# Retention and a SwiGLU block in float32 on one core: ring tiles named once and kept, in place of a new tile at every turn

## The chip, the core and the metric

The kernel runs on one core of a Trainium2 chip. A core has five engines with instruction streams of their own: TensorE (PE; its weight loads are listed as PEld), VectorE (DVE), ScalarE (ACT), GpSimd (POOL) and SyncE (SP), which here issues nearly all DMA transfers. [...] The metric is the device time of one execution in microseconds; smaller is better. The kernel before takes 652.57 us, the median of 3 runs (651.63 to 652.96).

## The reference

Two computations follow each other. The first is a retention recurrence over 4 batches, 8 heads, 768 positions and 64 columns per head; its output is turned into 3072 rows of 512 columns, which the second, a SwiGLU block with 1536 inner columns, takes as x.

```python
def _attn_ref(q, k, v):                      # q, k, v: (4, 8, 768, 64)
    gamma = 1.0 - 2.0 ** (-5.0 - np.arange(H, dtype=np.float32))
    scale = 1.0 / np.sqrt(D)
    for t in range(S):
        state = gamma[None, :, None, None] * state + np.einsum('bhd,bhe->bhde', k[:, :, t], v[:, :, t])
        y[:, :, t] = scale * np.einsum('bhd,bhde->bhe', q[:, :, t], state)

def _moe_ref(x, w_gate, w_val, w_out):       # x: (3072, 512)
    g = x @ w_gate                           # (512, 1536)
    silu = g * (1.0 / (1.0 + np.exp(-g)))
    val = x @ w_val
    return (silu * val @ w_out).astype(np.float32)   # w_out: (1536, 512)
```

Everything is float32.

## The kernel before

**Segments.** The 3072 rows are worked in four segments of 768 rows: three chunks of 128 rows for each of two batches. A segment has an up stage (x times the gate and value weights, 12 steps f of 128 inner columns, whose results go to `hT`) and a down stage (hT times `w_out`, 12 steps f of six matmul groups, one per chunk, accumulated in six PSUM banks). In the down stage of a segment the retention of the next one is computed as well: its matmuls stand between the groups of the down projection (L766), and its results are written into the next segment's x. Segment 0 is different: its retention runs first (to about 31 us), its up stage multiplies plainly (`plain`, L891 to L898, and `plain_part` for the first two steps), and beside it the weights are brought in, changed and stored in device memory in the form in which segments 1 to 3 load them (L490, L567, L1120).

**Splits.** TensorE multiplies in the type float32r. So that little is lost, every operand is split into three parts that are added again by three times as many matmuls. One split is three instructions on three engines. For weights and hT they are `near_a` (ScalarE, L967: part 0 from x), `near_b` (VectorE, L970: part 1 from part 0 and x) and `near_c` (part 2 from parts 0 and 1; GpSimd, L973; for hT VectorE, L407, by the function `both`). For x and the weights `w_out` in segment 0 they are `far_a` (L976), `far_b` (L979 on GpSimd, or L407) and `far_c` (L983). The matmuls run over the parts in the order 0, 1, 2.

**The products of the later segments.** In segments 1 to 3 the up stage of one f is seven products (`up3`, L1066): one product is part 0, 1, 2 with two matmuls each (L1060 to L1064), and the seven use seven sums of weights, in three groups of three, three and one (`GROUPS`). A group is one split: two of 768 columns in a tile of the ring "g" and one of 256 columns in a tile of the ring "o". Between the products ScalarE copies banks (L1077 to L1079) before the next product writes to them, and computes the silu (L1078, L1081).

**The rings.** `item` (L955) gives the tile into which a split goes:

```python
    k = turns[kind]
    turns[kind] += 1
    slots = {"g": 4, "o": 3}[kind]
    t = place(f"{kind}item{k}", {"g": 3 * 2 * TH, "o": 3 * DM}[kind], R12,
              tag=f"{kind}{k % slots}")
```

`place` (L409) makes a tile. A tile with the tag of an earlier one gets the same bytes, and what first writes to the new tile waits for all accesses to the old one, of whatever part. Ring "g" has four buffers of 3 x 768 columns, ring "o" three of 3 x 512. In the trace all tiles of a ring are called `gitem` or `oitem`. Users are `near_0` (L877, segment 0's up stage, 512 columns per part), `group` (L1036), `h_split` (L1089, hT, 768 columns per part) and `w_load` (L1102, the weights `w_out`: a DMA of part 2 in segment 0, L1107, followed by far_a to far_c, and of all three parts later, L1109). One call with `other` puts a tile of 3 x 512 over buffer g2. The buffers g0 to g3 hold raw weights (`rawp`) earlier in segment 0.

**x.** The split x of a segment lies in two tiles with the tags "xa" (four sums) and "xb" (three). Segment 0's x is the tile x0 over "xa"; `first`, over "xb", holds changed weights. `begin_x` (L990) makes two new tiles for each later segment:

```python
    xs_of[s] = [place(f"{n}{s}", 3 * o * KH * TH, R12, tag=n).rearrange(
        "p (a o k t) -> p a o k t", a=3, o=o, k=KH) for n, o in (("xa", 4), ("xb", 3))]
```

**Order.** Each piece of work is registered with a key and a due time (`at`, L448), but the order in which the instructions are issued is a list written out by hand, `PLAN` (L50 to L236), which `run` (L452) follows key by key. So each engine's instruction order is fixed; an engine runs its own in this order, and one that waits holds back what stands behind it on that engine.

Of the kernel before, what the change touches and what calls it, by code (L numbers as in the profile page):

```python
# [11 lines left out]
R12 = mybir.dt.float32r  # L12
# [9 lines left out]
DM = H * D  # L22
DFF = 1536
NC = DM // P
NF = DFF // P
L = 3
TH = L * P
NSEG = B * NCK // (2 * L)
KH = NC // 2
# [347 lines left out]
def tile_retnet_swiglu(  # L377
# [31 lines left out]
    def place(name, n, dtype=F32, **kw):  # L409
        return consts.tile([P, n], dtype, name=name, **kw)  # L410

    def f32(t):
        return t.bitcast(F32)

    XA, XB = 3 * 4 * KH * TH, 3 * 3 * KH * TH
    UNIT = 7 * KH * P
    hT = consts.tile([P, NF, 2, TH], F32, name="hT")
    X0 = place("x0", XA, R12, tag="xa").rearrange(
        "p (a i c t) -> p a i c t", a=3, i=2, c=NC)
    first = place("first", XB, tag="xb")  # L420
    rawp = {i: place(f"rawp{i}", 3 * 2 * TH, tag=f"g{i}") for i in (0, 1, 3)}
    loads = place("loads", 3 * UNIT + 256)
# [287 lines left out]
    def x_of(c):  # L710
        i, j = c // NCK % 2, c % L
        return [X0[:, a, i, :, ts(j, P)] for a in range(3)]

# [163 lines left out]
    def near_0(f, n):  # L877
        kind, part = divmod(n, 3)
        if part == 0:
            near_w[f, kind] = item("o", DM, (f, kind) == (1, 1))  # L880
        o = near_w[f, kind]
        o = [o[:, i] for i in range(3)]
        x = wt[f][:, ds(B22 if kind else B21, 2)].rearrange("p a b -> p (a b)")
        if part == 0:
            near_a(o, x)
        elif part == 1:
            near_b(o, x)
        else:
            near_c(o)

    def plain(f, kind, i):  # L891
        o = banks[2 * kind + i][:, :TH]
        w = near_w[f, kind]
        for a in range(3):
            for b in range(NC):
                nc.tensor.matmul(o, w[:, a, ts(b, P)], X0[:, a, i, NC - 1 - b],  # L896
                                 start=a == b == 0, stop=a == 2 and b == NC - 1,
# [11 lines left out]
    def plain_part(f, j, kind):  # L909
        o = part_of(f, j)[0][kind]  # L910
        w = near_w[f, kind]
        for a in range(3):
            for b in range(NC):
                nc.tensor.matmul(o, w[:, a, ts(b, P)], X0[:, a, :, NC - 1 - b, ts(j, P)],  # L914
                                 start=a == b == 0, stop=a == 2 and b == NC - 1,
# [35 lines left out]


    turns = {"g": 0, "o": 0}

    def item(kind, n, other=False):  # L955
        if other:
            t = place("oitem", 3 * DM, R12, tag="g2")
            return t.rearrange("p (a b) -> p a b", a=3)
        k = turns[kind]
        turns[kind] += 1  # L960
        slots = {"g": 4, "o": 3}[kind]
        t = place(f"{kind}item{k}", {"g": 3 * 2 * TH, "o": 3 * DM}[kind], R12,
                  tag=f"{kind}{k % slots}")
        return t[:, : 3 * n].rearrange("p (a b) -> p a b", a=3)

    def near_a(o, x):
        act(o[0], x, AF.Copy, scale=CUT / FAR)  # L967
# [17 lines left out]
    xs_of = {}  # L985
# [2 lines left out]
    st_x = tmp[:, ds(4 * TA, 4 * KH * P)].rearrange("p (m k t) -> p m k t", m=4, k=KH)  # L988

    def begin_x(s):  # L990
        xs_of[s] = [place(f"{n}{s}", 3 * o * KH * TH, R12, tag=n).rearrange(
            "p (a o k t) -> p a o k t", a=3, o=o, k=KH) for n, o in (("xa", 4), ("xb", 3))]

    def bring_y(z, h, i, c):
        y = banks[R0 + c][half[h], ds((2 * z + i) * 2 * HC, 2 * HC)]
# [40 lines left out]
    def group(f, g):  # L1036
        a, n = GROUPS[g]
        n *= KH * P
        src = blocks[f % 3][:, ds(a * KH * P, n)]
        o = ups[f, g] = item("o" if g == 2 else "g", n)  # L1040
        return [o[:, i] for i in range(3)], src
# [47 lines left out]
    def h_split(s, t, f, when):  # L1089
        it = {}  # L1090

        def begin():
            hs[f] = item("g", 2 * TH)
            it["o"] = [hs[f][:, i] for i in range(3)]
            near_a(it["o"], hT[:, f].rearrange("p i t -> p (i t)"))

        a, b, c = when
        at(t + a, f"{s}/h{f}.0", begin)
        at(t + b, f"{s}/h{f}.1", lambda: near_b(it["o"], hT[:, f].rearrange("p i t -> p (i t)")))
        at(t + c, f"{s}/h{f}.2", lambda: near_c(it["o"], pool if s == 0 and f in BY_POOL else both))  # L1100
# [59 lines left out]
    def down_stage(s, t):  # L1160
# [3 lines left out]
        for n in range(6 * NF):  # L1164
# [4 lines left out]
            if nxt and n in PARTS:  # L1169
                what, p = PARTS[n]  # L1170
                d = t + COST[what] + 0.1
                if what == "s":
                    at(t, f"{nxt}/sc{p}", scores_of, p, (R0, R0 + 1) if p else (4, 5))
                    for i in range(2):
                        at(d + 0.1 * i, f"{nxt}/dec{p}.{i}", decayed, p, i)
                        at(d + 0.2 + 0.1 * i, f"{nxt}/q{p}.{i}", scale_q2, p, i)
                    if has_old(nxt, p, 0):
                        at(d + 0.6, f"{nxt}/was{p}.0", decay2, nxt, p, 0)
                    if p == 0:
                        at(d + 0.7, f"{nxt}/begin", begin_x, nxt)  # L1180
                else:
                    k = "ABC".index(what)
                    z = k // 2
                    for i in range(0 if k else 2):
                        at(t - 0.02 + 0.01 * i, f"{nxt}/k{p}.{i}", scale_k2, p, i)
                    at(t, f"{nxt}/{what}{p}", (mix_a, mix_b, mix_c)[k], nxt, p)
                    if k != 1 and has_new(nxt, p, z):
                        at(d, f"{nxt}/new{p}.{z}", keep_state, nxt, p, z)
                    if k == 1 and has_new(nxt, p, 1):
                        at(d + 0.9, f"{nxt}/was{p}.1", decay2, nxt, p, 1)  # L1190
                    for j in range(8 if k else 0):
                        at(d + 0.1 * j, f"{nxt}/y{p}.{z}{j}", bring_y, z, j % 2, j // 2 % 2, j // 4)
                    if k == 2:
                        make_x(d + 1.0, nxt, p, table)
                t += COST[what]
# [44 lines left out]
    t = down_stage(0, end)  # L1240
    for s in range(1, NSEG):
# [8 lines left out]
        t = down_stage(s, t)  # L1250
# [50 lines left out]
```

## Time and profile before

| what | value |
|---|---|
| median of 3 runs | 652.57 us (651.63 to 652.96) |
| the profiled execution, its own time | 652.16 us |
| its span, first to last instruction | 650.4 us |
| mean granted TensorE clock | 0.997 |
| L1062, products of segments 1 to 3 | 1512 matmuls |
| L1125, down projection | 864 matmuls, 208.7 us |
| L896, plain up stage of segment 0 | 480 matmuls, 84.6 us |
| L967 ScalarE near_a | 847 ns (768 columns), 420 (256), 632 (512) |
| DMA read / written | 109.32 / 29.88 MB |

By stretches of the span, in us (busy time of the engines, share of the DMA engines):

| stretch | PE | DVE | ACT | POOL | DMA |
|---|---|---|---|---|---|
| 0 to 31 (segment 0's retention) | 25.93 | 20.29 | 16.30 | 9.57 | 1.00 |
| 31 to 118 (its up stage) | 87.00 | 71.49 | 70.49 | 42.74 | 0.90 |
| 118 to 165 (down stage begins) | 44.53 | 41.08 | 32.32 | 19.06 | 0.82 |
| 165 to 254 (rest of it, then segment 1 up) | 87.16 | 78.63 | 54.22 | 53.32 | 0.60 |
| 254 to 305 (segment 1 up) | 51.00 | 34.19 | 29.10 | 23.52 | 0.56 |
| 535 to 650 (segment 3, up and down) | 111.29 | 67.77 | 44.16 | 35.85 | 0.40 |

A row of the page's list of groups reads: line, engine, operation, output<-inputs by the names of the tiles, shape, count; busy time in us and the mean of one in ns; the engine's idle time just before these instructions and what ended most of it. A row of the timeline reads: start, duration, engine, line, operation, and in brackets the idle time before it and its releaser. Matmuls are pipelined: their starts are measured, their ends are modelled, so that in a steady stream each starts before the one ahead has ended.

### The profile page before, as it was taken

What the parts mean: (1) busy time and instruction counts of PE and PEld (TensorE: products, weight loads), DVE (VectorE), ACT (ScalarE), POOL (GpSimd) and SP (SyncE); (2) the same over time, 40 slices, a digit from 0 to 9 for tenths busy, and PEclk for the clock granted to TensorE, in tenths of its full rate; (3) what the DMA queues carried; (4) which work ended last, traced back from release to release, by engine and by line L of the source; (5) the groups of instructions that cost most, each with busy time, mean ns of one, the idle gap of its engine ahead of it and who ended that gap; (6) DMA issues with size and microseconds to landing.
All of it is one profiled execution on the core that took longest, in us unless ns stands there. A gap on an engine that the chain in (4) does not pass through costs nothing.

```text
span 650.4 us, 14042 instructions
## 1 busy us (share of the span) xinstructions
PE 636.1 (98%) x5576; PEld 579.8 (89%) x5576; DVE 490.3 (75%) x712; ACT 389.5 (60%) x860; POOL 270.9 (42%) x174
## 2 busy tenths in 40 slices
PE   7999999998989999999999999999999999999997
PEld 6899999987769999997878999998777999999886
DVE  4888688798898887675787959767598776778361
ACT  4688788577845555565766555656686554654221
POOL 0544347534445676730102666550003766562000
PEclk8999999999999999999999999999999999999999
DMA  9999898498757544157865540548677444304564
GB/s 325 374 350 336 323 348 283 165 360 283 276 183 302 201 146 166 38 195 261 260 237 205 191 152 20 187 132 294 203 270 264 150 158 163 117 4 157 177 216 147
DMA packets 50050, 140.13 MB, mean 215 GB/s; under 512 B 4928, under 2 KB 17472, under 8 KB 49984
## 3 DMA queue, kind: packets, MB, share of 16 engines
q1 hardware_dynamic: 49552, 138.57, 61.9%
q8 instruction: 44, 0.72, 0.4%
q10 hardware_dynamic: 432, 0.66, 0.3%
q14 instruction: 22, 0.18, 0.1%
HBM read 109.32 MB, written 29.88 MB: 214 GB/s over the span
## 4 chain that ended last, share of the span: by engine, by line
PE 91%; DVE 3%; DMA 2%; ACT 2%; POOL 1%; issue 1%; SPq 0%; ACTq 0%; DVEq 0%; POOLq 0%
PE bank L1062 40%; PE bank L1125 29%; PE bank L896 12%; PE bank L766 5%; PE bank L914 3%; DMA rawp<-in_w_gate_dram 1%; PE bank L636 1%; PE bank L707 1%; ACT chunk_x L996 1%; PE bank L721 1%; POOL oitem L973 1%; PE bank L692 1%; DMA loads<-in_k_n_dram 0%; POOL gitem L973 0%; DMA oitem<-wdn 0%
## 5 line engine op out<-in xcount | busy, mean ns | idle before, releaser
L1125 PE MATMUL bank<-oitem,gitem 128*128 128x512 f32 x864 | 208.7, 395 | 3.2 <-DVE oitem L983 2.9
L1125 PEld LDWEIGHTS bank<-oitem,gitem 128*128 128x128 f32 x864 | 159.3, 188 | 38.6 <-DVE oitem L983 4.4
L973 POOL TENSOR_TENSOR gitem<-gitem 128x768 fp32r<-128x768 f32 x72 | 143.4, 2001 | 105.2 <-DVE gitem L970 102.5
L1062 PE MATMUL bank<-xa,gitem 128*128 128x384 f32 x864 | 162.1, 336 | 0.6 <-ACT tmp L1078 0.3
L1062 PEld LDWEIGHTS bank<-xa,gitem 128*128 128x128 f32 x864 | 150.4, 188 | 3.0 <-ACT tmp L1077 2.2
L973 POOL TENSOR_TENSOR oitem<-oitem 128x256 fp32r<-128x256 f32 (+1 forms) x60 | 66.6, 1114 | 72.3 <-DVE oitem L970 63.7
L970 DVE SCALAR_TENSOR_TENSOR gitem<-gitem,loads 128x768 fp32r<-128x768 f32 x72 | 80.8, 1138 | 13.9 <-ACT gitem L967 10.0
L967 ACT ACTIVATE gitem<-loads 128x768 fp32r<-128x768 f32 x72 | 59.3, 843 | 50.8 <-PE bank L1062 39.3
L1062 PE MATMUL bank<-xb,gitem 128*128 128x384 f32 x432 | 85.4, 335 | 0.1
L896 PE MATMUL bank<-x,oitem 128*128 128x384 f32 x480 | 84.6, 336 | 0.8 <-POOL oitem L973 0.8
L896 PEld LDWEIGHTS bank<-x,oitem 128*128 128x128 f32 x480 | 83.0, 188 | 1.5 <-POOL oitem L973 1.1
L1062 PEld LDWEIGHTS bank<-xb,gitem 128*128 128x128 f32 x432 | 75.9, 188 | 1.0 <-POOL gitem L973 0.6
L970 DVE SCALAR_TENSOR_TENSOR gitem<-gitem,hT 128x768 fp32r<-128x768 f32 x48 | 48.3, 1012 | 26.7 <-ACT gitem L967 26.6
L967 ACT ACTIVATE gitem<-hT 128x768 fp32r<-128x768 f32 x48 | 39.9, 839 | 41.0 <-PE bank L1125 33.4
L996 ACT COPY chunk_x<-bank 64x128 f32<-64x128 f32 x144 | 35.4, 260 | 31.3 <-PE bank L766 17.9
L793 POOL TENSOR_TENSOR loads<-loads,tab 128x512 f32<-128x512 f32 x9 | 13.7, 1522 | 90.9 <-PE bank L766 90.9
L407 DVE SCALAR_TENSOR_TENSOR gitem<-gitem 128x768 fp32r<-128x768 f32 x48 | 46.8, 982 | 0.6
L1062 PE MATMUL bank<-xb,oitem 128*128 128x384 f32 x216 | 43.7, 337 | 0.0
L1062 PEld LDWEIGHTS bank<-xb,oitem 128*128 128x128 f32 x216 | 37.9, 188 | 0.4 <-POOL oitem L973 0.2
L970 DVE SCALAR_TENSOR_TENSOR oitem<-oitem,loads 128x256 fp32r<-128x256 f32 (+1 forms) x42 | 32.8, 786 | 3.7 <-ACT oitem L967 3.6
L979 POOL TENSOR_TENSOR oitem<-oitem 128x512 fp32r<-128x512 f32 x12 | 20.7, 1730 | 28.6 <-ACT oitem L976 28.6
L1079 DVE TENSOR_TENSOR hT<-bank,tmp 128x384 f32<-128x384 f32 x36 | 19.9, 553 | 14.6 <-PE bank L1062 14.6
(112 smaller groups left out, 788.3 us busy)
## 6 DMA issues: line engine op xcount, KB each, us to landing
loads<-wup SPq DMA_DIRECT2D x36, 896.0 KB, 4.7
oitem<-wdnt SPq DMA_DIRECT2D x36, 768.0 KB, 4.4
wdnt<-oitem SPq DMA_DIRECT2D x12, 768.0 KB, 4.6
wup<-first SPq DMA_DIRECT2D x9, 896.0 KB, 5.8
rawp<-in_w_gate_dram SPq DMA_DIRECT2D x12, 512.0 KB, 6.5
rawp<-in_w_val_dram SPq DMA_DIRECT2D x12, 512.0 KB, 5.6
rawp<-in_w_out_dram SPq DMA_DIRECT2D x12, 512.0 KB, 5.7
out_dram<-chunk_x SPq DMA_DIRECT2D x22, 256.0 KB, 2.3
```

Of the source, the lines that this page charges most:

```text
L407: stt(o, x, 1.0, y, op0=mul, op1=op)
L766: nc.tensor.matmul(o, a, b, start=start, stop=True, skip_group_check=True)
L896: nc.tensor.matmul(o, w[:, a, ts(b, P)], X0[:, a, i, NC - 1 - b], start=a == b == 0, stop=a == 2 and b == NC - 1, skip_group_check=True)
L914: nc.tensor.matmul(o, w[:, a, ts(b, P)], X0[:, a, :, NC - 1 - b, ts(j, P)], start=a == b == 0, stop=a == 2 and b == NC - 1, skip_group_che ...
L967: act(o[0], x, AF.Copy, scale=CUT / FAR)
L970: stt(o[1], f32(o[0]), -FAR, x, op0=mul, op1=add)
L973: op(o[2], f32(o[0]), f32(o[1]), op=add)
L979: op(o[1], f32(o[0]), x, op=sub)
L996: copy(cx[half[i], ds(2 * h, 2), c, half[z]], y.rearrange("p (b t) -> p b t", b=2))
L1062: nc.tensor.matmul(o, w[:, a, k], x[:, a, KH - 1 - k], start=start and a == k == 0, stop=a == 2 and k == KH - 1, skip_group_check=True)
L1079: lambda: copy(p5, wb), lambda: tt(h1, x, p5, op=add),
L1125: nc.tensor.matmul(banks[tok], hs[f][:, a, ds(i * TH + u * P, P)], wo[f][:, a], start=f == a == 0, stop=f == NF - 1 and a == 2, skip_group ...
```

## The change

`item` keeps a dictionary `slots` of the tiles it has made, by tag and size. The first turn of each buffer makes a tile; every later turn returns the same tile, cut to the columns asked for. The ring order (four and three buffers, and g2 for `other`) and the bytes are as before. The tile of the tag "xa" is made once, before segment 0, and kept in the list `xab`; the tile "xb" is made at the first `begin_x`, over `first`, and kept as well; `begin_x` then only cuts the two into the views of the segment. No arithmetic, no transfer and no entry of `PLAN` changes. What changes with it is what a first writer's waits go by: accesses to the same bytes of a tile that lives on, in place of the end of all use of the tile that was there before.

```diff
@@ -415,8 +415,8 @@
     hT = consts.tile([P, NF, 2, TH], F32, name="hT")
-    X0 = place("x0", XA, R12, tag="xa").rearrange(
-        "p (a i c t) -> p a i c t", a=3, i=2, c=NC)
+    xab = [place("xa", XA, R12)]
+    X0 = xab[0].rearrange("p (a i c t) -> p a i c t", a=3, i=2, c=NC)
     first = place("first", XB, tag="xb")
@@ -951,17 +951,18 @@
     turns = {"g": 0, "o": 0}
+    slots = {}
 
     def item(kind, n, other=False):
-        if other:
-            t = place("oitem", 3 * DM, R12, tag="g2")
-            return t.rearrange("p (a b) -> p a b", a=3)
-        k = turns[kind]
-        turns[kind] += 1
-        slots = {"g": 4, "o": 3}[kind]
-        t = place(f"{kind}item{k}", {"g": 3 * 2 * TH, "o": 3 * DM}[kind], R12,
-                  tag=f"{kind}{k % slots}")
-        return t[:, : 3 * n].rearrange("p (a b) -> p a b", a=3)
+        k = 2
+        if not other:
+            k = turns[kind] % {"g": 4, "o": 3}[kind]
+            turns[kind] += 1
+        size = {"g": 3 * 2 * TH, "o": 3 * (n if other else DM)}[kind]
+        tag = f"g{k}" if other else f"{kind}{k}"
+        if (tag, size) not in slots:
+            slots[tag, size] = place(f"{kind}item{k}", size, R12, tag=tag)
+        return slots[tag, size][:, : 3 * n].rearrange("p (a b) -> p a b", a=3)
@@ -988,8 +989,10 @@
     def begin_x(s):
-        xs_of[s] = [place(f"{n}{s}", 3 * o * KH * TH, R12, tag=n).rearrange(
-            "p (a o k t) -> p a o k t", a=3, o=o, k=KH) for n, o in (("xa", 4), ("xb", 3))]
+        if len(xab) == 1:
+            xab.append(place("xb", XB, R12, tag="xb"))
+        xs_of[s] = [t.rearrange("p (a o k t) -> p a o k t", a=3, o=o, k=KH)
+                    for t, o in zip(xab, (4, 3))]
```

## The prediction

> **What bounds the kernel now.** I read the page first, then who waited for whom, then the timeline around each place where TensorE steps late. The page:
>
> ```profile
> PE 636.1 (98%) x5576; PEld 579.8 (89%) x5576; DVE 490.3 (75%) x712; ACT 389.5 (60%) x860; POOL 270.9 (42%) x174
> ...
> L973 POOL TENSOR_TENSOR oitem<-oitem 128x256 fp32r<-128x256 f32 (+1 forms) x60 | 66.6, 1114 | 72.3 <-DVE oitem L970 63.7
> L970 DVE SCALAR_TENSOR_TENSOR gitem<-gitem,loads 128x768 fp32r<-128x768 f32 x72 | 80.8, 1138 | 13.9 <-ACT gitem L967 10.0
> L967 ACT ACTIVATE gitem<-loads 128x768 fp32r<-128x768 f32 x72 | 59.3, 843 | 50.8 <-PE bank L1062 39.3
> ```
>
> TensorE is busy for 636.1 of 650.4 us, so all that any change of waits can win is in the other 14.3 us and in matmuls that run late inside "busy" (their ends are modelled). ScalarE, VectorE and GpSimd have room. The last row shows what the change touches: ScalarE's first step of a split (near_a, L967) is idle for 50.8 us before its 72 instructions, mostly for TensorE. The waits, as engine and line, what was waited for, us in total, times, longest:
>
> ```profile
> ACT gitem L967 <- PE bank L1062: 41.6, 27, 3.7
> ACT gitem L967 <- PE bank L1125: 37.0, 17, 4.6
> ...
> ACT oitem L967 <- PE bank L896: 6.9, 6, 1.8
> ```
>
> In 50 cases near_a stands until a matmul has ended. It reads hT, `loads` or `first`, none of them written by TensorE, so what it waits for is room: the tile that had its buffer before must have been read for the last time. Whether that matters is decided by what is queued behind near_a on ScalarE. One place, in order of time:
>
> ```profile
> 510.10 2.07 PE L1062 MATMUL bank<-xa,gitem 128*128 128x384 f32 x11
> ...
> 511.21 0.85 ACT L967 ACTIVATE gitem<-loads 128x768 fp32r<-128x768 f32 x1 [1.31 <-PE bank L1062]
> ...
> 511.97 0.46 ACT L1078 COPY tmp<-bank 128x384 f32<-128x384 f32 x1
> 512.32 0.48 ACT L1079 COPY tmp<-bank 128x384 f32<-128x384 f32 x1
> 512.48 0.47 PEld L1062 LDWEIGHTS bank<-xa,gitem 128*128 128x128 f32 x3 [0.63 <-ACT tmp L1078]
> 512.48 0.62 PE L1062 MATMUL bank<-xa,gitem 128*128 128x384 f32 x2 [0.31 <-ACT tmp L1078]
> ```
>
> near_a starts at 511.21, 0.09 us after the last matmul on the old tile ended (511.13), and the copy that empties the bank (L1078) stands behind it until 511.97. TensorE needs that bank and starts at 512.48 in place of about 512.01. Consecutive matmuls of this line start 0.173 us apart (median); this one came 0.64 us after the one before, and the next 0.28. So the place costs 0.47 + 0.11 = 0.58 us, the 0.11 being a restart that follows every such wait.
>
> **The change part by part.** *Weights and hT (gitem, oitem).* Before, each turn is a new tile over the old one, and its first writer waits for the last access of the old tile whatever part it touched. Kept tiles have their history by the bytes: near_a writes part 0 and needs only the readers of part 0. A product runs part 0, 1, 2 with two matmuls each (L1060 to L1064), so the last reader of part 0 is four matmuls earlier: 4 x 0.173 = 0.69 us. In the down projection (L1125) it is two, 2 x 0.227 = 0.45 us, and in segment 0 (L896, four per part) eight, 8 x 0.173 = 1.39 us. For each near_a that the records show waiting for such a matmul, I took the latest of the earlier reader's end, ScalarE's instruction before and its other waits: some 60 of them could start earlier, by 36 us in total, 0.6 us at the mean. None of this is yet time. It becomes time only where TensorE stalls behind it.
>
> I followed every step of TensorE in these lines that is over 60 ns late back along its releases. Nine have a waiting near_a in the chain (time of the start; stall + restart, us): 125.64: 0.93 + 0.10; 216.47: 0.24 + 0.11; 232.71: 0.17 + 0.10; 248.60: 0.15 + 0.11; 392.91: 0.17 + 0.10; 512.48: 0.47 + 0.11; 538.83: 0.18 + 0.10; 546.66: 0.42 + 0.11; 590.99: 0.18 + 0.11. For the eight after 200 us the head start of 0.3 to 0.7 us is more than the stall, and what is next in the way is the end of the product that the copy reads: at 232.71 near_a moves from 230.71 to 230.02, a second near_a follows it, and the copy L1077, at 232.19 now, could start at 231.75, 0.09 after its product, which ends at 231.66. That is 0.44 earlier for a stall of 0.17. Sum of the eight: 2.83 us.
>
> The first is a longer chain:
>
> ```profile
> 118.67 6.21 PE L896 MATMUL bank<-x,oitem 128*128 128x384 f32 x34
> ...
> 119.27 0.63 ACT L967 ACTIVATE oitem<-loads 128x512 fp32r<-128x512 f32 x1 [1.78 <-PE bank L896]
> ...
> 119.94 0.69 DVE L970 SCALAR_TENSOR_TENSOR oitem<-oitem,loads 128x512 fp32r<-128x512 f32 x1 [2.40 <-ACT oitem L967]
> ...
> 120.66 2.59 DVE L407 SCALAR_TENSOR_TENSOR loads<-loads 128x512 f32<-128x512 f32 x3
> 120.71 1.80 POOL L973 TENSOR_TENSOR oitem<-oitem 128x512 fp32r<-128x512 f32 x1 [3.99 <-DVE oitem L970]
> ...
> 123.17 0.68 DVE L970 SCALAR_TENSOR_TENSOR oitem<-oitem,loads 128x512 fp32r<-128x512 f32 x1
> ...
> 123.94 1.66 POOL L973 TENSOR_TENSOR oitem<-oitem 128x512 fp32r<-128x512 f32 x1 [1.43 <-DVE oitem L970]
> 125.64 0.64 PEld L896 LDWEIGHTS bank<-x,oitem 128*128 128x128 f32 x4 [1.08 <-POOL oitem L973]
> 125.64 0.79 PE L896 MATMUL bank<-x,oitem 128*128 128x384 f32 x3 [0.77 <-POOL oitem L973]
> ```
>
> VectorE is idle for 2.40 us until near_a has run, then works without a gap to 123.86, and GpSimd's part 2 of the last weight ends at 125.59. near_a could start at 117.88, 1.39 earlier, and the chain with it, so the 1.03 us could go. But the down projection of segment 0 follows, at 0.82 DMA share between 118 and 165 us, and its first weight load (L1107, issued at 123.73 behind a reader that does not move) feeds ScalarE at 128.26 and GpSimd until 131.47; VectorE takes that result at 132.81, so 1.34 us are spare there, yet later loads may give some back. Between 0 and 1.03 I take 0.6.
>
> *The waits that are added.* near_b (VectorE, part 1) and near_c (part 2; GpSimd, for hT VectorE) now have readers of their own to wait for, due later than near_a's by a third and two thirds of a product's remainder. For 768 columns: 0.35 and 0.69 us, while near_a itself takes 0.843, so it hides both. For 256 columns: near_a 0.42 and near_b 0.41 against 0.35 and 0.69, hidden. For 512 in segment 0: 0.69 and 1.39 against 0.63 + 0.09 and 0.69 more, just hidden; without that cover VectorE would stand up to 0.35 us, and the hT additions (L1079 to L1081) behind it. As instructions: a wait beyond the first stands in a semaphore instruction of its own. Where such a wait had long been met, the start after the instruction before (which overlaps by the modelled pipeline) came at -79 ns against -82 without it on VectorE, -94 and -94 on ScalarE, -39 and -39 on GpSimd: 0 to 3 ns, and 200 of them cost at most 0.6 us of engines that are idle a quarter of the time. On TensorE more matmuls must report their end; after those that report now the next starts 173 ns later at the median, after the others 174. Cost 0, bounds 0 to 0.1 us.
>
> *x (xa, xb).* The earlier segment's last matmul on xb ends at 291.8, the first write for the next is at 308.9 (445.1 and 467.3 for the one after; x0 134.2, first write to xa1 159.0): at least 17 us apart, so nothing waits and nothing is won. *W loads* write part 2 or all parts; their last reader is the old one: nothing. *The tile over g2* is used once.
>
> Sum: 2.83 + 0.6 = 3.4 us. The profiled execution took 652.16 (650.4 span, 1.8 around it), 0.41 under the median of the runs: **648.8 us**.
>
> **The rivals.** *More.* Segment 0's down projection also stalls at 157.80 (1.85 us), 180.76 and 187.46 (1.36) behind VectorE. If earlier splits loosen these, another 1 to 3 us go: about 646. Against it: VectorE works without a gap from 148.79 to 160.7, started by copies that follow TensorE, and no near_a waits there. *Nothing.* If the dependencies of a kept tile are still taken whole, or near_a's wait goes to the next matmul that reports, all stays: 652.2. For it: nothing in the trace of before shows a kept tile with three parts being rewritten while read; `tmp` and `loads` are rewritten in pieces, and there L1077 starts without regard to the pieces beside it. *Slower: VectorE and GpSimd collide.* L970 on 768 columns takes 0.945 us at the least and 1.890 at the most in segment 1's up stage; the slow ones run beside GpSimd's L973 (1.87). An earlier near_b can move from a free stretch into one of these, 0.945 us late, then near_c and TensorE behind it. Slack on VectorE between 254 and 305 us is 51.0 - 34.2 = 16.8, 2.4 us for each of its seven steps of 7.3, so most are absorbed; if one in six of the 36 steps of the later segments paid 0.945 on TensorE's path, 5.7 us would be lost: 652.2 - 3.4 + 5.7 = 654.5. Four such eat the gain, five or six make it slower by a measurable amount. Against it: in the whole up stages only one stall, at 216.47, ends on GpSimd, and none on VectorE's L970. [...]
>
> **How the numbers follow.** A measurement tells 0.2% (1.3 us) from no change. Chances: forecast (2 to 5 us won) 0.62, more 0.06, nothing or less than 1.3 either way 0.21, slower 0.11 (collisions 0.08, the rest unknown). Faster by over 0.2% is then 0.68. The range goes down to 646.8 (3.86 whole, half a microsecond of five lone restarts of 0.11, 1 us of the first rival) and up to 652.4, into the case of nothing; below and above are left some 0.05 and 0.13.
>
> **What would show it.** Right: near_a's idle before its release by L1062 falls by about 0.6 us each, from 41.6 us; the starts at 512.48 and 546.66 lose their waits for ScalarE; VectorE's near_b at 119.94 comes over a microsecond earlier and 125.64 follows the matmul before it. Wrong: L967 still starts 0.09 us behind the product's last matmul (nothing), or L970's mean rises well over 1138 ns while PEld waits for VectorE or GpSimd (slower). What would upset the sum itself is a stall that moves to a place that near_a never reached.

## The result and the profile after

| | before | after |
|---|---|---|
| median, executions in turn on one chip | 653.36 us (651.63 to 655.14, 12) | 649.13 us (648.11 to 652.34, 12) |
| ratio of after to before | | 0.9941, 95% interval 0.9926 to 0.9955 |
| the profiled execution, its span | 652.16, 650.4 us | 652.34, 650.5 us |
| L1062, now L1065, near_a idle for it | 41.6 us in 27 waits | 24.8 us in 21 waits |

The change takes 0.6% off, some 4 us. Ratios are of fast executions alone; one execution of experiment 9, at 2193.21 us, is left out of its ratio. The profiled execution of the changed kernel is its slowest of the twelve: before 458.31 us TensorE stands for 2.70 us, in a place that has nothing to do with the rings, and its granted clock is one half for 6.83 us around that place (the last section). Times of stages are therefore read from a second profile of the same, unaltered kernel (experiment 10, 648.84 us); the idle times of near_a (31.8 us) and near_b (7.5) below are the same in both.

The line numbers move by one to three: near_a is L968, near_b L971, near_c L974, the products L1065, the copies L1080 to L1082. The rows of the page that answer to those shown of before, from the list of groups of the kernel after (idle time and its releaser at the end):

```profile
L974 POOL TENSOR_TENSOR oitem<-oitem 128x256 fp32r<-128x256 f32 (+1 forms) x60 | 67.7, 1132 | 70.1 <-DVE oitem L971 56.1
L971 DVE SCALAR_TENSOR_TENSOR gitem<-gitem,loads 128x768 fp32r<-128x768 f32 x72 | 81.1, 1143 | 7.5 <-ACT gitem L968 5.8
L968 ACT ACTIVATE gitem<-loads 128x768 fp32r<-128x768 f32 x72 | 59.2, 842 | 31.8 <-PE bank L1065 24.4
```

near_a's idle time went from 50.8 to 31.8 us and near_b's from 13.9 to 7.5, while near_b's mean, 1143 ns against 1138, did not rise. Who waited for whom, in the kernel after (total us, times, longest):

```profile
ACT gitem L968 <- PE bank L1128: 39.7, 15, 7.1
...
ACT gitem L968 <- PE bank L1065: 24.8, 21, 3.0
...
POOL gitem L974 <- PE bank L1065: 15.1, 9, 4.5
...
ACT oitem L968 <- PE bank L896: 2.1, 3, 1.5
```

The waits for the products fell by 16.8 us, 0.62 for each of the 27, and those for segment 0's up stage from 6.9 to 2.1. Counted in matmuls, 20 of the 24 splits of weights from `loads` that waited for a product start exactly four matmuls earlier than before. The waits for the down projection hardly moved: the first row holds the long stall at 458, and in the second profile it is 35.9 us, against 37.0 before, although 11 of 14 splits of hT start two matmuls earlier there; the work ahead of each wait comes earlier too. The third row had been this in the list before:

```profile
POOL gitem L973 <- PE bank L1062: 2.8, 1, 2.8
```

near_c now waits nine times and not once, since it has readers of its own part to wait for. The place that the prediction took as its example, in order of time, in the kernel after:

```profile
511.97 4.34 PE L1065 MATMUL bank<-xa,gitem 128*128 128x384 f32 x23
...
512.84 0.85 ACT L968 ACTIVATE gitem<-loads 128x768 fp32r<-128x768 f32 x1 [1.34 <-POOL gitem L974]
513.59 0.46 ACT L1081 COPY tmp<-bank 128x384 f32<-128x384 f32 x1
...
514.10 2.06 PEld L1065 LDWEIGHTS bank<-xa,gitem 128*128 128x128 f32 x12 [0.21 <-ACT tmp L1081]
514.25 0.48 ACT L1082 COPY tmp<-bank 128x384 f32<-128x384 f32 x1 [0.20 <-PE bank L1065]
```

The pair of products on xa starts at 511.97 here, and in the profile of before at 509.93:

```profile
509.93 2.24 PE L1062 MATMUL bank<-xa,gitem 128*128 128x384 f32 x12
```

From there the two can be laid side by side. near_a came 1.28 us behind that start (511.21 - 509.93) and comes 0.87 behind it now (512.84 - 511.97); the copy behind it came at 2.04 and comes at 1.62, and the 23 matmuls run on as one row where TensorE stood until 2.55 before. The head start is 0.41 us and not the 0.69 of four matmuls: the wait that ends last now is, by the profile, for GpSimd's near_c. That is nearly all of the 0.47 that was lost there: TensorE comes 0.06 us late at 514.11, and a restart of 0.11 is left at 514.39.

The other chain, at the end of segment 0's up stage, in the kernel after:

```profile
117.62 0.63 ACT L968 ACTIVATE oitem<-loads 128x512 fp32r<-128x512 f32 x1 [0.39 <-PE bank L896]
...
118.31 0.69 DVE L971 SCALAR_TENSOR_TENSOR oitem<-oitem,loads 128x512 fp32r<-128x512 f32 x1 [1.04 <-ACT oitem L968]
...
119.03 2.60 DVE L407 SCALAR_TENSOR_TENSOR loads<-loads 128x512 f32<-128x512 f32 x3
...
121.55 0.68 DVE L971 SCALAR_TENSOR_TENSOR oitem<-oitem,loads 128x512 fp32r<-128x512 f32 x1
...
122.31 1.68 POOL L974 TENSOR_TENSOR oitem<-oitem 128x512 fp32r<-128x512 f32 x1 [1.43 <-DVE oitem L971]
```

near_b's idle time there is 1.04 us in place of 2.40, and all that follows on VectorE without a gap comes with it: GpSimd's last part ends at 123.99, or 77.61 us after the first matmul of L896 (at 46.38), against 125.60 - 46.65 = 78.95 before. TensorE no longer stands in front of it.

From the start of every TensorE matmul come the lengths of the stages, from the first matmul of one to the first of the next (us; segment 0's up stage from the first matmul of L896, the last stage to the start of its last matmul):

| stage | before | after (second profile) | difference | the prediction's terms |
|---|---|---|---|---|
| segment 0 up | 87.36 | 86.15 | -1.21 | -1.03 |
| segment 0 down | 67.98 | 67.14 | -0.83 | +0.43 |
| segment 1 up | 89.66 | 88.99 | -0.67 | -0.88 |
| segment 1 down | 60.81 | 61.02 | +0.21 | 0 |
| segment 2 up | 89.47 | 89.15 | -0.32 | -0.27 |
| segment 2 down, without the stall at 458 | 62.70 | 62.72 | +0.02 | 0 |
| segment 3 up | 91.29 | 89.37 | -1.92 | -1.68 |
| segment 3 down | 49.85 | 49.85 | 0.00 | 0 |
| sum | | | -4.72 | -3.43 |

The stall at 458 was 0.42 us in the profile before and 1.87 in the second profile after. It varies from execution to execution and is left out of the row; that the medians differ by 4.2 and the stages by 4.7 is within it. Of the 0.21 of segment 1's down stage, 0.18 are a stall of 0.07 and its restart of 0.11 at 314.

### The profile page after: what moved, and what is told of

Read it like the earlier page. It is cut to its first block, busy times and chain, and to the rows that moved or that the text cites. A ratio compares the mean times of both kernels' runs of the same rounds, so it can differ in the third digit from the quotient of the medians.

```text
span 650.5 us, 14090 instructions
## 1 busy us (share of the span) xinstructions
PE 635.7 (98%) x5576; PEld 581.5 (89%) x5576; DVE 489.6 (75%) x712; ACT 392.4 (60%) x860; POOL 272.3 (42%) x174
## 4 chain that ended last, share of the span: by engine, by line
PE 89%; DMA 4%; DVE 3%; ACT 2%; issue 1%; SPq 0%; ACTq 0%; DVEq 0%
PE bank L1065 40%; PE bank L1128 27%; PE bank L896 13%; PE bank L766 5%; PE bank L914 2%; DMA rawp<-in_w_gate_dram 1%; ACT chunk_x L999 1%; DMA hT<-in_k_n_dram 1%; DMA hT<-in_q_t_dram 1%; DVE oitem L984 0%; DMA loads<-in_v_n_dram 0%; DVE xb L407 0%; PE bank L721 0%; ACT states L865 0%; DVE tmp L407 0%
## 5 line engine op out<-in xcount | busy, mean ns | idle before, releaser
L1128 PE MATMUL bank<-oitem,gitem 128*128 128x512 f32 x864 | 210.9, 398 | 5.6 <-DVE oitem L984 2.9
L1128 PEld LDWEIGHTS bank<-oitem,gitem 128*128 128x128 f32 x864 | 160.5, 189 | 41.8 <-DVE oitem L984 4.4
L974 POOL TENSOR_TENSOR gitem<-gitem 128x768 fp32r<-128x768 f32 x72 | 143.7, 2005 | 100.7 <-DVE gitem L971 74.2
L1065 PE MATMUL bank<-xa,gitem 128*128 128x384 f32 x864 | 160.7, 334 | 0.0
L1065 PEld LDWEIGHTS bank<-xa,gitem 128*128 128x128 f32 x864 | 150.8, 188 | 0.3 <-ACT tmp L1081 0.2
L974 POOL TENSOR_TENSOR oitem<-oitem 128x256 fp32r<-128x256 f32 (+1 forms) x60 | 67.7, 1132 | 70.1 <-DVE oitem L971 56.1
L971 DVE SCALAR_TENSOR_TENSOR gitem<-gitem,loads 128x768 fp32r<-128x768 f32 x72 | 81.1, 1143 | 7.5 <-ACT gitem L968 5.8
L1065 PE MATMUL bank<-xb,gitem 128*128 128x384 f32 x432 | 85.2, 335 | 0.0
L896 PE MATMUL bank<-xa,oitem 128*128 128x384 f32 x480 | 84.2, 335 | 0.0
L896 PEld LDWEIGHTS bank<-xa,oitem 128*128 128x128 f32 x480 | 83.0, 188 | 0.2
L968 ACT ACTIVATE gitem<-loads 128x768 fp32r<-128x768 f32 x72 | 59.2, 842 | 31.8 <-PE bank L1065 24.4
L1065 PEld LDWEIGHTS bank<-xb,gitem 128*128 128x128 f32 x432 | 76.0, 188 | 0.7 <-POOL gitem L974 0.3
L971 DVE SCALAR_TENSOR_TENSOR gitem<-gitem,hT 128x768 fp32r<-128x768 f32 x48 | 50.3, 1053 | 30.1 <-ACT gitem L968 30.0
L968 ACT ACTIVATE gitem<-hT 128x768 fp32r<-128x768 f32 x48 | 40.0, 840 | 41.1 <-PE bank L1128 37.5
L793 POOL TENSOR_TENSOR loads<-loads,tab 128x512 f32<-128x512 f32 x9 | 13.7, 1517 | 98.6 <-PE bank L766 83.1
L407 DVE SCALAR_TENSOR_TENSOR gitem<-gitem 128x768 fp32r<-128x768 f32 x48 | 45.9, 962 | 1.1
L1065 PE MATMUL bank<-xb,oitem 128*128 128x384 f32 x216 | 43.6, 336 | 0.0
L1065 PEld LDWEIGHTS bank<-xb,oitem 128*128 128x128 f32 x216 | 37.9, 188 | 0.2
L971 DVE SCALAR_TENSOR_TENSOR oitem<-oitem,loads 128x256 fp32r<-128x256 f32 (+1 forms) x42 | 32.5, 780 | 2.3 <-ACT oitem L968 2.2
L1080 ACT COPY tmp<-bank 128x384 f32<-128x384 f32 x36 | 17.2, 478 | 25.6 <-PE bank L1065 21.4
```

The lines of the kernel that those rows point to most:

```text
L407: stt(o, x, 1.0, y, op0=mul, op1=op)
L793: (pool if i else both)(t, t, qdec, op=mul)
L971: stt(o[1], f32(o[0]), -FAR, x, op0=mul, op1=add)
L974: op(o[2], f32(o[0]), f32(o[1]), op=add)
L1065: nc.tensor.matmul(o, w[:, a, k], x[:, a, KH - 1 - k], start=start and a == k == 0, stop=a == 2 and k == KH - 1, skip_group_check=True)
L1080: steps = (lambda: copy(p1, x), lambda: tt(c11, z, p1, op=add), lambda: act(gate, c11, AF.Silu, scale=ONE), lambda: copy(u2, x), lambda: c ...
```

## The experiments

Each was timed against the kernel before in turn with it; a ratio under 1 is faster than before. "Stall" is the time by which a TensorE matmul starts later than its regular step.

**1. Only x kept.** `xab` and `begin_x` as in the change, the rings as before.

```diff
-    X0 = place("x0", XA, R12, tag="xa").rearrange(
+    xab = [place("xa", XA, R12)]
+    X0 = xab[0].rearrange("p (a i c t) -> p a i c t", a=3, i=2, c=NC)
...
+        if len(xab) == 1:
+            xab.append(place("xb", XB, R12, tag="xb"))
```

> Only the two tiles of x are kept; gitem and oitem are new tiles at every turn as before. Theory A (the gain is near_a starting when part 0 of its buffer has been read): no change against before, ratio 1.000 within 0.0015, because the last read of x and the first write of the next lie 17 us or more apart. Theory B (fewer tiles and releases save work by themselves, wherever they are): a part of the gain, some 0.999. Theory C (the gain is in x): 0.994.

Measured: 653.35 us against 653.62, ratio 0.9996 (0.998 to 1.0012). All nine stalls of before are there, from the one of 0.91 us at 125.3 to those at 548.2 and 592.5 (546.66 and 590.99 before). Keeping x changes nothing that can be told.

**2. Only ring "g" kept** (768 columns, and hT).

```diff
-        t = place(f"{kind}item{k}", {"g": 3 * 2 * TH, "o": 3 * DM}[kind], R12,
-                  tag=f"{kind}{k % slots}")
+        if kind != "g" or (kind, k) not in slots:
+            slots[kind, k] = place(f"{kind}item{turns[kind]}", size, R12, tag=f"{kind}{k}")
```

> Only the four buffers of ring g are kept. Theory A: the stalls at 216, 232, 392, 512, 538, 546 and 591 us go (2.57 us by the profile before), those at 125.6 and 248.6, which stand behind an oitem, stay: 652.16 - 2.6 = 649.6 for the profiled time, ratio 0.996. Theory B: by the number of tiles kept (120 of 180), two thirds of the gain everywhere, also at 125.6: 0.996, told from A by the 125.6 us stall alone.

Measured: 649.66 us, ratio 0.9937 (0.992 to 0.9954). Of the nine stalls the first (0.92, here at 126.8) and the one at 248.6 (0.14) stay, 0.07 is left of the one at 216, and the others are gone. More was won than the 0.996 foreseen: the stall at 180.8, which is not among the nine, went as well. By its regular step it is 0.46 us; the retention's matmuls in which it stands take 0.87 us less without it (experiment 11).

**3. Only ring "o" kept** (256 columns, segment 0's 512, and `w_out`): the same line with `kind != "o"`.

> Only the three buffers of ring o are kept. Theory A: the stalls at 125.6 (1.03 us) and 248.6 (0.26) go, the other seven stay: 1.3 us, ratio 0.998. Theory B: one third of the gain, 0.998, spread over all places: the stall at 125.6 would shrink, not vanish.

Measured: 651.94 us, ratio 0.9975 (0.9963 to 0.9987). As expected, the stalls at 125.6 and 248.6 are gone; the seven others stay, and so does the one at 180 (0.46). In stage lengths, the stall at 458 left out, ring "g" alone is worth 3.52 us and ring "o" alone 1.45, together 4.97, against 4.72 for both: two almost separate halves, and every stall of the nine goes with the ring of its near_a.

**4. All kept, but part 0 read last.** In the kernel after, a product runs over the parts 1, 2, 0. The sums are the same in another order.

```diff
-        for a in range(3):
+        for j, a in enumerate((1, 2, 0)):
             for k in range(KH):
                 nc.tensor.matmul(o, w[:, a, k], x[:, a, KH - 1 - k],
-                                 start=start and a == k == 0, stop=a == 2 and k == KH - 1,
+                                 start=start and j == k == 0, stop=j == 2 and k == KH - 1,
```

> All tiles kept as in the changed kernel, but the products of segments 1 to 3 run the parts in the order 1, 2, 0, so that part 0 is read last and near_a has again to wait for a product's last matmul. The sums in PSUM are taken in another order, nothing is left out. Theory A: the head start in the up stages of segments 1 to 3 is gone and their stalls come back, L968 waits for L1065 some 40 us again; only the 1.0 us at 125.6 is kept: ratio to before 0.998. Theory B (keeping saves by itself): 0.994 as in the changed kernel.

Measured: 651.80 us, ratio 0.9972 (0.9959 to 0.9985). The waits of near_a for the products, in this kernel:

```profile
ACT gitem L968 <- PE bank L1065: 38.6, 24, 3.7
```

38.6 us, close to the 41.6 of before and not to the 24.8 of after, with tiles that are kept all the same. The stalls are back at 214.6 (0.72), 231.2 (0.17), 247.0 (0.15), 391.5 (0.17), 511.4 (0.75), 537.8 (0.18), 545.6 (0.42) and 590.1 (0.07), some longer than before, and 196.0 (0.66) and 578.7 (0.37) are new. Part 2, which is made last, is needed two matmuls sooner in this order, and those at 214.6 and 578.7 are released by GpSimd's near_c; those at 231, 247, 391, 538 and 546, with the copy behind near_a in their chain, are of the size of before. Segment 3's up stage takes 91.75 us, 0.46 more than before. The one at 125.6, behind segment 0's plain matmuls, whose order is as it was, stays away. Of the 24 splits counted above, 23 start at the same matmul as in the kernel before. So the gain of the later segments is the release of part 0 ahead of the rest; that a tile is kept does not bring it by itself.

**5. The kernel before, with copies issued ahead of near_a.** Seven places in the hand-written order: where a bank's copy (u) stood behind a waiting near_a (w, h), it goes ahead of it. No tile is kept.

```diff
-1/w5.0.0 1/p4.0 1/u3.6 1/p3.6 1/u4.0
+1/p4.0 1/u3.6 1/p3.6 1/u4.0 1/w5.0.0
...
-1/w7.0.0 1/w7.2.1 1/w7.0.1 1/p6.3 1/w7.2.2 1/u6.0
+1/u6.0 1/w7.0.0 1/w7.2.1 1/w7.0.1 1/p6.3 1/w7.2.2
```

> The kernel before, every tile new at every turn as there; only the order of ScalarE's work is changed at seven places: the copy that empties a bank (u0.3, u4.0, u5.0, u6.0, u11.0 of segments 1 to 3) is issued ahead of the waiting near_a that stood before it. Theory A with its second half (the time is lost because the copy stands behind near_a on ScalarE, not because near_a itself is late): the stalls at 232, 248, 392, 512, 538, 546 and 591 us go without any tile being kept, 2.5 us, ratio 0.996; those at 125.6 and 216, which go through VectorE and GpSimd, stay. If a late near_a is what costs, whatever stands behind it: 1.000.

Measured: 651.57 us against 653.13, ratio 0.9976 (0.9962 to 0.9989). All stalls of the seven places are gone; those at 125.2 (0.93), 180.3 (0.48) and 216.0 (0.21) stay, and one comes up at 253.5 (0.53). With it the gain is some 1.6 us, less than the 2.5 expected. The waits of near_a in this kernel (L958 is near_a and L1053 the products):

```profile
ACT gitem L958 <- PE bank L1053: 37.3, 26, 3.7
```

near_a still stands for 37.3 us, nearly as long as before, and at the seven places TensorE does not. There its idle time costs nothing by itself; what cost time was the copy queued behind it.

**6. After, with four entries of segment 0's down stage moved** (part 2 of a `w_out`, `0/d4.2`, ahead of a write of x, as shown; and three writes of x, `1/x1.0.0`, `1/x1.1.1` and `1/x1.1.2`, behind `0/d9.0` and `0/d9.2`).

```diff
-1/x0.1.2 1/sc1 1/dec1.1 0/D3.2 1/q1.1 1/sum0.2 1/l6 1/dec1.0 0/D3.4 1/q1.0 0/D3.1 0/W5 0/D3.3 0/d4.2
+0/d4.2 1/x0.1.2 1/sc1 1/dec1.1 0/D3.2 1/q1.1 1/sum0.2 1/l6 1/dec1.0 0/D3.4 1/q1.0 0/D3.1 0/W5 0/D3.3
```

> The changed kernel with four entries of the order list moved in segment 0's down stage, where VectorE is the late engine: the last step of weight 4 of the down projection (d4.2) two steps earlier, and three steps of x (x1.0.0, x1.1.1, x1.1.2) behind the last steps of weight 9. The stall at 156.2 (1.85 us in the changed kernel's trace) should go wholly, of that at 185.2 (1.36) about 1 us: ratio to before 0.990, against 0.994 without. If VectorE only shifts its backlog to the next need (the score masks of L789, the x split), the stalls return within 10 us and the ratio stays at 0.994.

Measured: 649.88 us, ratio 0.9953 (0.9931 to 0.9975), not told apart from the change alone. The stalls at 156 (1.85) and 185 (1.36) are gone and come back at 168.6 (1.88), 195.0 (0.58), 195.9 (0.66) and, in the stage after, 214.3 (0.32): the stage takes 67.23 us in place of 67.14.

**7. After, with the seven moves of experiment 5.**

> All tiles kept, and in the hand-written order the seven copies of e5 issued ahead of the near_a that they stood behind. Theory A (both edits work on the same stalls: the copy behind a waiting near_a): not additive, the time of the kept tiles alone, ratio 0.994 to the kernel before, 649.3 us. Theory B (keeping the tiles does something else as well, the two gains add up): 0.994 x 0.998 = 0.991, 647.7 us. No stall at 231, 391, 512, 538, 546, 590 in either.

Measured: 649.13 us against 652.97, ratio 0.9933 (0.9918 to 0.9948). In the same series the change alone (experiment 10) gives 0.9934. No further gain shows within the interval, as expected if both take away the same stalls by two means; the two gains added would have been 0.991. The stall at 252.0 (0.53) that experiment 5 brought is here too, so it belongs to the moves.

**8. and 9. After, with two and with four moves in segment 0's down stage.** The first moves `0/d4.2` as in 6 and `1/x0.0.2` behind `0/d6.2`, as shown; the second also moves `1/x1.1.1` and `1/x1.1.2` behind `0/d9.2`.

```diff
-1/x0.0.2 1/C1 0/d7.0 0/h7.1 0/h7.2 1/y1.17 0/Z5 0/d6.2
+1/C1 0/d7.0 0/h7.1 0/h7.2 1/y1.17 0/Z5 0/d6.2 1/x0.0.2
```

> All tiles kept; in segment 0's down stage one addition of hT parts (VectorE) is issued ahead of one write of the next x, and one write of x later, so that the matmuls at 156.2 (stall 1.85 us) and 185.2 (1.36) need not wait behind it. If these two stalls are a matter of order alone, up to 3.2 us go: ratio 0.989 to 0.992, segment 0's down stage 64 to 65.7 us in place of 67.2. If VectorE is behind by its whole backlog there, the stalls come back a few us later, as in e6 (67.23): ratio 0.994.

> As e8, and two further writes of x behind the last hT addition of f 9. If the stall at 185 is set by what stands just ahead of it: 1 us better than e8, 0.990. If the backlog decides: as e8 or slightly worse, with new stalls at 195 (the writes of x now late for the first products), 0.994.

Measured: 649.14 us, ratio 0.9939 (0.9924 to 0.9955), and 649.88 us (the median of five), ratio 0.9945 (0.9929 to 0.9961). In 8 the stall at 156 becomes 1.16 + 0.78 at 178 and 179, and 1.36 at 185.7 stays (stage 67.51 us); in 9 the last becomes 0.94, and 0.66 at 198.0 and 0.35 at 216 follow (68.02 us). (The entries `0/d` are parts of `w_out`; the two expectations call them additions of hT.) Three different orders move the 3.2 us and none shortens the stage. It looks as if VectorE had that much work too many in front of TensorE, and as if the order only decided which matmul pays; the three orders do not prove it. In the experiments 4, 11 and 12 the stall of 1.36 shrank to 0.27 or 0.28, and one of 0.66 followed at 195 to 198 us.

**10. The change once more.**

> The changed kernel once more, unaltered, for the size of the gain on this chip and a second profile. Expected 0.994 (0.9926 to 0.9955 before); stalls at 156.2 (1.85) and 185.2 (1.36), none at 125, 180, 231, 247, 391, 512, 538, 546, 590. At about 458 us a stall whose length is the run's own: 0.4 to 4 us, and where it is under 2.5 us no stretch of half clock behind it; the span is then 645.5 to 648 us.

Measured: 648.82 us (648.47 to 650.37) against 652.97, ratio 0.9934 (0.992 to 0.9949). Stalls at 156.4 (1.85), 185.4 (1.35), 329.0 (0.36) and 457.5 (1.87), which the kernel before has as well; at the nine places only 0.11 and a restart of 0.10 at 214.3, the place of 216.47, and one of 0.07 at 314 that is new.

**11. The kernel before, with two sums and one part of x ahead of a part of w_out.** This is about the stall at 180.8, which the prediction had not counted. VectorE and GpSimd in the kernel before:

```profile
174.83 0.42 DVE L407 SCALAR_TENSOR_TENSOR xb<-xb,chunk_x 128x256 fp32r<-128x256 f32 x1
175.11 1.30 POOL L793 TENSOR_TENSOR loads<-loads,tab 128x512 f32<-128x512 f32 x1 [3.83 <-PE bank L766]
175.17 1.52 DVE L407 SCALAR_TENSOR_TENSOR tmp<-tmp,chunk_x 128x256 f32<-128x256 f32 x1
...
178.33 0.68 DVE L789 TENSOR_TENSOR tmp<-bank,local 128x512 f32<-128x512 f32 x1
```

and in the second profile of the kernel after:

```profile
173.35 0.42 DVE L407 SCALAR_TENSOR_TENSOR xb<-xb,chunk_x 128x256 fp32r<-128x256 f32 x1
173.69 0.42 DVE L407 SCALAR_TENSOR_TENSOR tmp<-tmp,chunk_x 128x256 f32<-128x256 f32 x1
173.72 1.54 POOL L793 TENSOR_TENSOR loads<-loads,tab 128x512 f32<-128x512 f32 x1 [3.87 <-PE bank L766]
...
176.00 0.68 DVE L789 TENSOR_TENSOR tmp<-bank,local 128x512 f32<-128x512 f32 x1
```

The same addition takes 1.52 us where it starts 0.06 behind GpSimd's L793, ending 0.28 after that one has ended, and 0.42 us where it starts 0.03 ahead; then L793 is the slower, 1.54 for 1.30. From there to L789 it is 3.16 us (178.33 - 175.17) against 2.31. A tenth of a microsecond decides over 0.85. The experiment lets the addition run early, in the kernel before:

```diff
-0/d7.2 0/D6.4 1/was2.0 0/W8 0/D6.5 1/l10 1/sc2 0/D6.3 1/sum1.2 0/D7.2 1/x1.2.1 1/sum1.1
+1/sum1.2 1/x1.2.1 1/sum1.1 0/d7.2 0/D6.4 1/was2.0 0/W8 0/D6.5 1/l10 1/sc2 0/D6.3 0/D7.2
```

> The kernel before; in segment 0's down stage two sums of x and one part of x (VectorE, L407 on 256 columns, 0.42 us each) are issued ahead of the part of w_out (L983, 0.68 us) that stood between them, so that the last sum starts some 0.6 us before GpSimd's L793 and not 0.09 us behind it. Theory (VectorE loses up to one GpSimd instruction when it starts behind it): this L407 takes 0.42 us in place of 1.52, VectorE's L789 follows some 0.85 us earlier, the stall at 180.8 (0.46 us) goes and segment 0's down stage takes 67.2 to 67.5 us in place of 67.98; the other stalls stay; ratio 0.9988. Rival (the stall went because splits were earlier, not by the collision): the stall at 180.8 stays, 67.9 us, ratio 1.000.

Measured, in this kernel (L398, L784 and L780 are the lines called L407, L793 and L789 above, and L974 is the part of `w_out`, L983 in the kernel before):

```profile
174.65 0.41 DVE L398 SCALAR_TENSOR_TENSOR tmp<-tmp,chunk_x 128x256 f32<-128x256 f32 x1
174.98 0.68 DVE L974 SCALAR_TENSOR_TENSOR oitem<-oitem 128x512 fp32r<-128x512 f32 x1
175.18 1.64 POOL L784 TENSOR_TENSOR loads<-loads,tab 128x512 f32<-128x512 f32 x1 [3.31 <-PE bank L757]
...
177.56 0.68 DVE L780 TENSOR_TENSOR tmp<-bank,local 128x512 f32<-128x512 f32 x1
```

The addition takes 0.41 us, and L780 follows 4.79 us after the L398 at 172.77 (5.64 before, from 172.69 to 178.33): 0.85 earlier, as expected. The stall at 180.8 is gone: the retention's matmuls there take 1.34 us (179.95 to 181.29) in place of 2.21 (179.87 to 182.09). The stage takes 67.08 us in place of 67.98 without any kept tile. Against the expectation the other stalls did not stay: new ones of 0.19 at 182.1 and 0.66 at 197.4 came, and the 1.36 at 187.5 shrank to 0.27, which about balance. In the whole time nothing can be told: 652.79 us against 653.23, ratio 1.000 (0.9988 to 1.0012). The 0.24 at 216 grew to 0.40 in the stage after.

**12. The same move on the kernel after.**

> The same move on the changed kernel, where this L407 already starts beside or ahead of GpSimd's L793 and takes 0.42 us. Theory: nothing more to win, segment 0's down stage 67.1 to 67.2 us, ratio to the kernel before 0.994. Rival (the order itself is better, whatever GpSimd does): another 0.3 to 0.8 us, ratio 0.993, stage 66.4 to 66.9.

Measured: 648.32 us, ratio 0.9926 (0.991 to 0.9942), the stage 66.90 us in place of 67.14. The interval holds the 0.9934 of the change alone: not told apart. By the stage the rival came in (66.4 to 66.9) and not the theory (67.1 to 67.2): here too the stall of 1.36 shrank, to 0.28, and one of 0.66 came at 195.6, so the order does a little of its own. The 0.24 us of the stage are lost again in the next (89.23 against 88.99). It has the lowest median of all kernels here, and no proof that it is a better one.

## Why the prediction was right, and where its sum was off

**The mechanism held.** near_a waited for the whole old tile, and keeping the tiles lets it go as soon as part 0 has been read. Experiment 4 is the proof: with the same kept tiles and part 0 read last, the waits return to 38.6 us and the stalls with them. Experiment 5 is the other half: at seven of the nine places what cost time was the copy behind near_a, since moving the copies alone takes these stalls away and leaves near_a its waits. Experiment 7 agrees, as the two gains do not add up; its interval is 0.3% wide.

**That the time came so near is partly luck.** 649.13 us against 648.8 hides two differences: in the series of the result the kernel before takes 653.36 us and not the 652.16 from which the sum started, and the gain was 4.2 us and not 3.4.

**The eight stalls after 200 us** were put at 2.83 us; the up stages of the segments 1 to 3 became shorter by 0.67 + 0.32 + 1.92 = 2.91. One by one: of 216.47 a tenth and the restart were left, and segment 3 gave a quarter of a microsecond more, as two lone restarts of 0.11 that are not in the sum, at 580.04 and 585.41, went too. The size was right.

**The term for segment 0 was mis-sized.** Of 1.03 us at 125.64 the prediction kept 0.6, expecting the down stage to give 0.43 back. The up stage gave 1.21 and the down stage took nothing back but gave 0.83 on top, so this term measured 2.04 us in place of 0.6. The fear that later loads of `w_out` would not follow was unfounded. The 0.83 came in the main from 180.76, which the prediction had named among the stalls of the rival "more" and set aside, since no near_a waits there. That reading was right as far as it went, though its other argument, VectorE's work without a gap from 148.79 to 160.7, bore on the stall at 157.80 alone, and that one stayed (1.85). What it missed is that a stall behind VectorE also depends on the order in which VectorE and GpSimd reach the same moment, and that shifting one by a tenth of a microsecond is enough (1.52 us where the addition starts 0.06 behind L793, 0.42 where it starts 0.03 ahead). Experiment 11 shows that a move which lets the addition run early, with no kept tile, makes the matmuls there 0.87 us shorter; that the kept ring "g" caused it by such a shift is read from the traces (experiment 2 has the fast addition, 1 and 3 the slow one), not from a run that separates the two.

**The added waits** cost nothing that the time shows. The 48 further wait instructions stand in the kernel's count (14090 against 14042), and near_c's waits for the products, 15.1 us in place of 2.8, hold up nothing that was seen: the one place of the nine where near_a now waits for GpSimd keeps a restart of 0.11 us.

**x, the loads and the tile over g2** were put at nothing; experiment 1 measured 0.9996 (0.998 to 1.0012) for x.

**The rivals.** "Nothing" fell with the waits for the products, 24.8 us in place of 41.6. "Slower by collisions" fell with near_b's mean of 1143 ns. Yet collisions there are, and of the kind that this rival priced: they went the other way, in segment 0's down stage. One of them cost VectorE more than the 0.945 us that the rival put for each: the addition that started at 175.17, beside GpSimd's L793, did not end before that one, which was over at 176.41, but 0.28 us behind it. It took 1.52 us where it takes 0.42 in the kernel after, 1.10 more, and 1.24 of L793 were left when it started. In the second profile of the kernel after, L793 started behind the addition, with 0.39 of it left, and took 1.54 us for 1.30, 0.24 longer; VectorE's L971 ran beside it from 174.03, so the 0.24 is not shown to be the addition's alone.

## What to carry to other kernels

A wait is worth what is queued behind it on the same engine and then stalls the bound engine: 41.6 us of near_a's waits were worth 3 us here, and seven copies moved ahead of it won part of that with the waits nearly as they were. Where a buffer is written and read in parts, a tile that is kept is released part by part in the order in which the readers use it, so the part that is written first should be read first (24.8 us of near_a's waits that way, 38.6 with it read last). An estimate made of stalls and releases can be good to a tenth of a microsecond for each and still miss a stage where two engines meet by chance; such a stage is better given a range of both signs than a discount.

## What the runs showed of the hardware that was not expected

A matmul of the down projection at about 458 us (L1125, L1128 after), the same one each time, starts late in all fourteen profiles, in kernels with and without the change, although the profile shows no engine and no tile that it waits for. The timeline of TensorE in the kernel after:

```profile
454.88 0.73 PE L1128 MATMUL bank<-oitem,gitem 128*128 128x512 f32 x2
458.31 4.42 PE L1128 MATMUL bank<-oitem,gitem 128*128 128x512 f32 x10 [2.70 <-issue]
```

The same place of the same profile by stretches (from and to, length, busy us and instructions of PE, PEld, DVE, ACT and POOL, granted clock, DMA share, GB/s):

```profile
455.00:458.00 3.00, 0.61 (x2) 0.36 (x3) 0.00 (x0) 2.89 (x12) 0.00 (x0) 0.91 0.17 47
458.00:461.00 3.00, 2.69 (x7) 2.10 (x7) 0.00 (x0) 0.37 (x2) 0.00 (x0) 0.50 0.02 5
461.00:468.00 7.00, 7.00 (x70) 5.38 (x69) 1.62 (x4) 1.89 (x5) 0.00 (x0) 0.76 0.26 80
```

The clock was half from 457.48 to 464.30. The timeline of TensorE there in the second profile of that kernel:

```profile
455.09 0.73 PE L1128 MATMUL bank<-oitem,gitem 128*128 128x512 f32 x2
457.53 1.78 PE L1128 MATMUL bank<-oitem,gitem 128*128 128x512 f32 x7 [1.71 <-issue]
```

"Issue" means that the profile shows nothing that the engine waited for. But each time a packet of 16 KB on the queue for instructions was under way (at 455.75 for 1.11 us in the first, at 455.15 for 1.12 in the second), and the matmul starts 1.2 to 1.7 us after the packet has landed, in all fourteen. That TensorE had run out of instructions is the author's reading of this and is not shown: no run here changes the instruction stream. The stall was 0.4 to 0.9 us in five profiles, 1.1 to 2.5 in seven, and 2.87 and 3.94 in two, and only in these two did the clock fall to one half there, for 6.83 us. An idle time of 2.70 us was followed by it in the kernel after, and one of 2.37 (experiment 12) was not. The stall is some of the spread between executions of one kernel, and a single profile can mislead by it: the profiled execution of experiment 5, with the stall of 3.94, took 655.91 us, and its median is 651.57.
